# A linear-attention and MLP kernel: crossbar transposes moved to TensorE, w_in loaded through GpSimd's DMA queue with the cast in the transfer

## The chip, the cores and the metric

The kernel runs on one core of a Trainium2 chip. A core has TensorE (matrix products, PE in the profile, with its weight loads as PEld), VectorE (DVE), ScalarE (ACT), GpSimd (POOL) and SyncE (SP), which here only issues DMA transfers. The engines run side by side, each through its own list of instructions in the written order, and wait for each other through semaphores. TensorE writes to PSUM, of which this kernel uses eight banks; VectorE and ScalarE copy results from there to SBUF. The metric is the time of one execution on the device in microseconds.

## The reference

Two parts follow each other. The first is a linear attention with decay, over 4 batches, 8 heads, 768 steps and 48 features per head:

```python
for t in range(S):
    cur = np.einsum('bhd,bhe->bhde', u[None] * kt, vt)
    y[:, :, t] = np.einsum('bhd,bhde->bhe', rt, state + cur)
    state = wt[:, :, :, None] * state + np.einsum('bhd,bhe->bhde', kt, vt)
```

The second takes the 3072 rows of 384 that come out, as x, through an MLP with 2048 hidden features:

```python
h = x @ w_in
r = np.maximum(h, 0.0)
g = s * (r * r) + b
return g @ w_out
```

Inputs and output are float32. The kernel does its matrix products in bf16.

## The kernel before, in words

The 768 steps of each batch are cut into 6 chunks of 128, so there are 24 chunks, numbered 0 to 23; the number goes through the batches first, then through the steps. Chunks 0 to 3 are loaded and worked on in pairs ("packed", pkt tiles), the others alone (wt, rkt, vt tiles). The steps of one chunk, by the names that the written order uses:

- load n.0 to n.3: w, r, k, v come in over SP's DMA queue.
- ln, cum, exp, inc, exn: logarithm of w (ScalarE), its running sum (TensorE, L410 and others), exponentials (ScalarE), with inc on VectorE.
- mul: the products prd of r and k with these exponentials (VectorE, L489).
- The turn of prd, so that features lie across partitions. tr and tev: TensorE makes eight 128 x 128 transposes into PSUM (L538), and ScalarE or VectorE copies them to the tile RK (function move, L552 and L554). Or tev alone: a transposing DMA on SP (dtrans, L575), called the crossbar in this document, which needs neither TensorE nor a copy. `xbar_rk(n)` and `xbar_x(n)` choose by thresholds.
- mt, msk: scores (TensorE, L617) and their triangular mask (VectorE, L629).
- rkp, rku, cd, yd: the diagonal term with u. Two products on GpSimd (L346, L352), a sum on VectorE (L369), a product on GpSimd (L375).
- vb: v in bf16, by whichever engine the order names.
- dmm, sup, l2, st: the new state. TensorE (L741), VectorE (L784), GpSimd (L525, L793).
- ymm, yev: the chunk's output (TensorE, L667 and L676; VectorE, L758), which is a part of x.
- The turn of x: xtr and xev (three transposes on TensorE, L804, and a copy), or xev alone as a transposing DMA (dxtr, L585).

Two chunks make a tile of 256 rows of x; there are 12 tiles. For each, eight groups g1 T.i of six matmuls make 256 hidden features at a time (L858), relu (ScalarE, L871) and sq (ScalarE L881, VectorE L883) make gT, and g2 T.q sums over the hidden features in groups of four matmuls (L901). oev scales and adds a row that comes from b and the column sums of w_out (L912), and store writes it out.

The weights come in five pieces of 2, 2, 4, 4 and 4 times 128 hidden features. Before the change a piece of w_in is loaded by SP into a float32 staging tile (load_win, L826; li in the order) and cast to bf16 by ScalarE (pieces 0, 1, 3 in the list CIE; the order overrides it) or another engine (cast_in; ci in the order; L981, L983, L985). w_out goes the same way (load_wout L838, co), and its float32 staging tiles are also summed over rows for the output's constant (csred, csadd, cssplit). Staging tiles are shared: three large ones and two half-sized, for w_in and w_out together.

What sets the order of the work is the text ORDER: one list of words for all engines, worked through from front to back. Each engine gets its instructions in the order in which its words stand there. A word such as sq3.1@A names the operation, the tile or chunk, the part, and the engine that takes it (A, D, P for ScalarE, VectorE, GpSimd). A number such as +9 stands for so many matmuls on zeros (L1286, "fillers"), which keep TensorE running in the opening. Each PSUM tile of the ring psP (six banks: sums, scores, transposes, outputs, states, hidden features) can be written again only when its reader is done. SP's list works the same way: a load that has to wait for a buffer holds up everything behind it.

Of the kernel before, what the change touches and what calls it, by code (L numbers as in the profile page):

```python
# [18 lines left out]
CIE = 'AAPAP'  # L19
# [8 lines left out]
DTK = 9  # L28
DTX = 18
DK2 = 24  # L30
DX2 = 24
# [10 lines left out]
load0.0 load0.2 +9 load0.1 ln0 load2.2 cum0.0 load0.3 cum1.0 exp0.0 +1 u_mm exp0.1 load2.0 exp1.0  # L42
rkp0 mul0.0 load2.1 cum1.1 mul0.1 exp1.1 rkp1 load4.0 u_ev@D tr0 mul1.0 +4 tev0@A mul1.1 rku1 li0
tr1 load2.3 exl0 +2 rku0 cd1 tev1@A li1 ln2 cd0 mt0 load4.1 msk1.0 cum2.0 rkp3 l21 li2 msk0.0 +2 yd1
ln4 exp2.0 cum3.0 cum3.1 msk0.1 l20 rku3 ci0@A load4.2 msk1.1 cum4.0 +3 vb0@D vb1@A yd0 mul2.0
exp2.1 lo0 dmm0 exp3.1 mul2.1 +2 li3 exp3.0 li4 exl2 mul3.0 exp4.0 l23 cum4.1 sup0 vb3@P ymm0.0
exp4.1 tr2 rkp2 ci1@A mul3.1 st0 ymm0.1 sup1 ydm0 vb2@A l24 lo1 rku2 ymi0 yev0@D tr3 yev1@A tev2@D
xtr0 tev3@A xtr1 l22 +1 st1 xev0@D cd2 xev1@A mt2 cd3 rkp4 ci2@A g10.0 msk3.0 yd3 g10.1 msk2.0
relu0.0 lo2 msk2.1 yd2 ymm2.0 relu0.1 g10.2 msk3.1 rku4 dmm2 mul4 relu0.2 ymm2.1 ydm2 co0@A ci3@P
g10.3 sq0.1@A sup2 yev2@A cd4 st2 ymi2 sq0.2@A xtr2 sup3 yev3@A csred0@D lo3 g10.4 sq0.0@A ci4@D  # L50
load5.0 xev2@A xtr3 g10.5 load6.0 relu0.3 co1@D xev3@A lo4 g10.6 csred1@D sq0.3@A load5.1 g11.0
relu0.6 csadd1@D g11.1 relu0.4 co2@D relu0.5 g20.0 csred2@D sq0.4@A g10.7 sq0.6@A g11.2 sq0.5@A
relu0.7 g11.3 csadd2@D relu1.0 load5.2 g20.1 co3@D relu1.3 g20.4 relu1.1 load6.1 csred3@D ln5 g20.5
ln6 tr4 sq0.7@A cum6.0 csadd3@P tev4@D cum5.0 relu1.2 g11.4 inc6 sq1.3@A load6.2 g11.5 sq1.0@A co4@D
cum5.1 exp5.0 g11.6 small2 csred4@D exp5.1 load5.3 exp6.0 g20.6 exn6 g11.7 relu1.6 mul5 relu1.4
small g20.7 sq1.1@A load4.3 csadd4@D g20.2 relu1.7 load7.0 cssplit tr5 sq1.2@A load8.0 relu1.5 mul6
csspread g20.3 csevac load8.1 tev5@D vb5@P tr6 sq1.5@A rkp5 oev0.0 tev6@A mt4 load9.0 oev0.1 g21.4
l25 msk4.0 sq1.4@A rku5 load7.1 dmm5 g21.0 vb4@A msk5.0 g21.5 ln7 load7.2 sup5 rkp6 sq1.7@A msk4.1
cum7.0 st5 yd4 dmm4 load8.2 g21.1 load9.1 ln8 exp7.0 sup4 l26 cum8.0 cd5 st4 ymm4 ln9 msk5.1 yd5
g21.6 sq1.6@A inc7 load6.3 ymm5 exp8.0 st3 yev4 cum9.0 exn7 g21.7 yev5 rku6 inc8 xtr4 xtr5 g21.2  # L60
xev4@A load10.0 mul7 l27 xev5@A g21.3 exn8 load9.2 inc9 rkp7 g12.0 oev1.1 exp9.0 load9.3 g12.1 mul8
relu2.0 l28 relu2.1 load7.3 g12.2 cd6 l29 sq2.1@A sq2.0@D yd6 g12.3 load11.0 tr7 load10.1 exn9
oev1.0 relu2.2 g12.4 tev7@D vb6@P relu2.3 load8.3 g12.5 relu2.4 sq2.3@D mul9 sq2.4@A mt6 relu2.5
g22.4 msk7.0 store0.0 sq2.2@A vb7@P g12.6 msk6.0 sq2.5@A rkp9 load11.1 tev9 msk6.1 dmm6 g22.0
relu2.6 rku7 ln10 sup6 g12.7 load10.2 ln11 msk7.1 tr8 rku9 relu2.7 cd7 g22.1 sq2.7@A cum10.0 cd9
tev8@A load12.1 vb9@A dmm7 ymm6 rkp8 inc10 g22.5 rku8 yev6 load12.0 cum11.0 sup7 g22.6 yd9 xtr6
# [103 lines left out]
def kernel(  # L170
# [650 lines left out]

    def load_win(i):
        fs, f0 = PIECES[i], F0[i]
        half = fs == 2
        st = wst.tile([128, KT, fs * 128], FP32, name="wi_st", tag="wsh" if half else "wst", bufs=2 if half else 3)
        nc.sync.dma_start(  # L826
            out=st,
# [159 lines left out]
    def cast_in(i):  # L987
        cast(("ci", i), w_in_sb[i], w_in_st[i])
# [338 lines left out]
```

## Time and profile before

| What | Value |
|---|---|
| Median of 3 runs | 183.34 us (183.16 to 183.92) |
| Profiled execution, its own time | 183.5 us |
| Span of the profiled execution | 181.7 us |
| TensorE busy | 171.8 us, 1874 matmuls |
| VectorE, ScalarE, GpSimd busy | 142.8, 142.2, 105.0 us |
| First-layer matmuls (L858) | 576, 70.9 us busy |
| Second-layer matmuls (L901) | 400, 71.8 us busy |
| Transposing DMAs | 15 of r and k, 6 of x |
| Transposes on TensorE | 72 of r and k (9 chunks), 54 of x (18 chunks) |

The span runs from the first instruction to the last; the execution's own time is some 1.8 us more. In the rows of the profile, a line number names the place in the kernel, then come engine, operation, output and inputs, shapes and counts. Busy times of matmuls overlap: 54 matmuls of 219 ns each did not hold TensorE for 54 times 219 ns. How long a group holds the engine is read from where the next one starts.

### The profile page before, as it was taken

Reading aid. Unit: us, or ns where it says so; the run is one execution under the profiler, and the core shown is the slowest. Engines: PE = TensorE matmul, PEld = TensorE weight load, DVE = VectorE, ACT = ScalarE, POOL = GpSimd, SP = SyncE. Lnnn points to the kernel's source line nnn. Section 1 sums busy time; section 2 is a strip of 40 time slices with the busy share of each in tenths; the row PEclk is TensorE's granted clock in tenths of the full one; section 3 lists DMA queues with packets and bytes.
Section 4 is the critical chain, followed back from the end, with each engine's and each line's share of the span. In section 5 each row is a group of like instructions: output and inputs, shape, how many; then the busy total and the mean of one; then the engine's idle time right before and its main releaser. Section 6 shows DMA issues by size and latency. Waiting matters only on the chain.

```text
span 181.7 us, 4868 instructions
## 1 busy us (share of the span) xinstructions
PE 171.8 (95%) x1874; PEld 131.9 (73%) x1876; DVE 142.8 (79%) x257; ACT 142.2 (78%) x279; POOL 105.0 (58%) x139
## 2 busy tenths in 40 slices
PE   7989879998999989999999999999999999999993
PEld 2455669765686769688689688787877696888762
DVE  7679999999999979798998497898998976330222
ACT  3589899998889559979878899898896188479920
POOL 3889860229599699559869759289809560000000
PEclk9999999999999999999999999999999999999999
DMA  5999999999898998999989889999994794220013
GB/s 154 323 324 343 387 350 274 260 184 206 167 207 178 187 187 182 199 171 183 232 186 195 212 172 202 208 199 243 160 206 100 158 238 153 69 60 11 0 43 132
DMA packets 116554, 34.72 MB, mean 191 GB/s; under 512 B 110898, under 2 KB 114739, under 8 KB 116531
## 3 DMA queue, kind: packets, MB, share of 16 engines
q1 hardware_dynamic: 116528, 34.42, 81.6%
q8 instruction: 14, 0.23, 0.5%
q14 instruction: 10, 0.07, 0.1%
q10 hardware_dynamic: 2, 0.00, 0.0%
HBM read 25.17 MB, written 4.72 MB: 164 GB/s over the span
## 4 chain that ended last, share of the span: by engine, by line
PE 64%; DVE 10%; DMA 7%; POOL 6%; issue 5%; ACT 4%; SPq 1%; DVEq 0%; ACTq 0%; POOLq 0%
PE o_ps L901 27%; PE h_ps L858 26%; DMA wo_st<-in_moe_w_out_dram 4%; DMA rkt<-in_k_dram 3%; PE mt_ps L617 2%; POOL rkp L346 2%; PE y_ps L676 2%; DVE prd L489 2%; PE y_ps L667 2%; POOL rku L352 1%; POOL yd L375 1%; PE d_ps L741 1%; ACT rh L871 1%; PE cums L410 1%; PE xt_ps L804 1%
## 5 line engine op out<-in xcount | busy, mean ns | idle before, releaser
L901 PE MATMUL o_ps<-w_out,gT 128*128 128x384 bf16 (+2 forms) x400 | 71.8, 320 | 0.5 <-ACT gT L881 0.5
L858 PE MATMUL h_ps<-xT,w_in 128*128 128x256 bf16 x576 | 70.9, 273 | 1.1 <-POOL w_in L983 0.6
L871 ACT ACTIVATE rh<-h_ps 128x512 bf16<-128x512 f32 x96 | 54.4, 597 | 16.6 <-PE h_ps L858 15.7
L858 PEld LDWEIGHTS <-w_in 128*128 128x128 bf16 x576 | 59.9, 110 | 6.1 <-issue 1.0
L901 PEld LDWEIGHTS <-gT 128*128 128x128 bf16 x400 | 36.1, 98 | 19.7 <-ACT gT L881 0.7
L881 ACT ACTIVATE gT<-rh 128x512 bf16<-128x512 bf16 x78 | 47.4, 634 | 0.5
L352 POOL TENSOR_TENSOR rku<-rkp,u_bc 128x384 f32<-128x384 f32 x24 | 27.7, 1158 | 2.2 <-DVE cd L369 1.6
L346 POOL TENSOR_TENSOR rkp<-rkt 128x384 f32<-128x384 f32 x20 | 21.3, 1068 | 11.2 <-DMA rkt<-in_k_dram 9.4
L629 DVE TENSOR_TENSOR mt_sb<-mt_ps,tri_strict 128x512 bf16<-128x512 f32 x40 | 25.4, 681 | 1.9 <-PE mt_ps L617 1.8
L375 POOL TENSOR_TENSOR yd<-vt,cd 128x384 bf16<-128x384 f32 x20 | 17.6, 884 | 11.0 <-DVE cd L369 10.7
L489 DVE TENSOR_TENSOR prd<-rkt,E 128x768 bf16<-128x768 f32 x20 | 23.7, 1187 | 0.3 <-ACT E L473 0.3
L912 DVE SCALAR_TENSOR_TENSOR o_sb<-o_ps,s_bc,bconst 128x384 f32<-128x384 f32 (+2 forms) x25 | 14.6, 594 | 6.4 <-PE o_ps L901 6.3
L883 DVE TENSOR_TENSOR gT<-rh 128x512 bf16<-128x512 bf16 x18 | 9.6, 536 | 10.2 <-ACT rh L871 10.2
L793 POOL TENSOR_TENSOR st<-stmp,l 128x384 bf16<-128x384 bf16 x16 | 15.5, 972 | 0.8 <-DVE stmp L784 0.8
L758 DVE TENSOR_TENSOR x_sb<-y_ps,yd 128x384 bf16<-128x384 f32 x20 | 10.7, 549 | 5.3 <-PE y_ps L676 5.2
L369 DVE TENSOR_REDUCE cd<-rku 128x8 f32<-128x384 f32 x24 | 12.8, 542 | 1.4 <-POOL rku L352 1.4
L448 ACT ACTIVATE E<-cums 128x388 f32<-128x388 f32 (+1 forms) x22 | 10.4, 496 | 4.3 <-DVE inc L463 2.4
L784 DVE TENSOR_TENSOR stmp<-d_ps,st 128x384 bf16<-128x384 f32 x16 | 8.7, 550 | 3.2 <-PE d_ps L741 3.1
L473 ACT ACTIVATE E<-inc 128x384 f32<-128x384 f32 x18 | 9.3, 525 | 1.5 <-DVE inc L463 1.4
L1286 PE MATMUL warm_ps<-warm_sb 128*128 128x512 bf16 x22 | 7.7, 477 | 1.3 <-DVE warm_sb L1242 1.2
L983 POOL CAST vb<-vt 128x384 bf16<-128x384 f32 x9 | 5.6, 629 | 4.1 <-DMA vt<-in_v_dram 4.1
L676 PE MATMUL y_ps<-vb,mt_sb 128*128 128x48 bf16 x160 | 7.3, 183 | 0.0
(112 smaller groups left out, 200.6 us busy)
## 6 DMA issues: line engine op xcount, KB each, us to landing
wt<-in_w_dram SPq DMA_DIRECT2D x20, 192.0 KB, 3.9
rkt<-in_r_dram SPq DMA_DIRECT2D x20, 192.0 KB, 3.8
rkt<-in_k_dram SPq DMA_DIRECT2D x20, 192.0 KB, 3.7
vt<-in_v_dram SPq DMA_DIRECT2D x20, 192.0 KB, 3.6
out_dram<-o_sb SPq DMA_DIRECT2D x19, 192.0 KB, 3.0
wi_st<-in_moe_w_in_dram SPq DMA_DIRECT2D x3, 768.0 KB, 7.5
wo_st<-in_moe_w_out_dram SPq DMA_DIRECT2D x3, 768.0 KB, 7.0
pkt<-in_w_dram SPq DMA_DIRECT2D x2, 384.0 KB, 4.1
```

The source lines that it names most:

```text
L346: nc.gpsimd.tensor_tensor(out=rkp, in0=c["r"], in1=c["k"], op=ALU.mult)
L352: nc.gpsimd.tensor_tensor(out=rku.rearrange("t h d -> t (h d)"), in0=c["rkp"].rearrange("t h d -> t (h d)"), in1=u_bc, op=ALU.mult,)
L369: nc.vector.reduce_sum(out=cd, in_=c["rku"], axis=AX.X)
L375: nc.gpsimd.tensor_tensor(out=yd, in0=c["v"], in1=c["cd"].unsqueeze(2).to_broadcast([128, H, D]), op=ALU.mult,)
L489: nc.vector.tensor_tensor(out=prd[:, :, :, 0:D], in0=c["rk"], in1=c["E"][:, :, 0:HD].rearrange("t x (h d) -> t x h d", h=H), op=ALU.mult,)
L629: nc.vector.tensor_tensor(out=c["mt"][:, sg], in0=c["mt_ps"][sg], in1=(masks[:, n % 2] if packed(n) else tri_strict) .unsqueeze(1) .to_bro ...
L793: nc.gpsimd.tensor_tensor(out=c["st_new"], in0=c["stmp"].rearrange("q p (g e) -> q p g e", g=2), in1=c["l2"].unsqueeze(3).to_broadcast([12 ...
L858: nc.tensor.matmul(ps[:, f, :], lhsT=w_in_sb[PIECE[ft]][:, kt, :].rearrange("p (m j) -> p j m", j=PIECES[PIECE[ft]])[:, ft - F0[PIECE[ft]] ...
L871: nc.scalar.activation(out=rh, in_=hs[T, i], func=AF.Relu)
L881: nc.scalar.activation(out=g, in_=rh, func=AF.Square)
L901: nc.tensor.matmul(os_[T, k][:, cols], lhsT=gT[T][:, ft, tt * 128 : (tt + 1) * 128], rhs=w_out_sb[PIECE[ft]][:, ft - F0[PIECE[ft]], cols], ...
L912: nc.vector.scalar_tensor_tensor(out=o_sb[:, cols], in0=os_.pop((T, k))[:, cols], scalar=s_bc, in1=bconst[:, cols], op0=ALU.mult, op1=ALU.add,
```

## The change

Three things change.

1. The four thresholds of the crossbar are set to 99, above every chunk's number. All 24 chunks have r and k turned by TensorE, and all 24 parts of x. The transposing DMAs are gone.
2. A piece of w_in is loaded by GpSimd's DMA queue straight into the bf16 tile, the turn to bf16 done in the transfer. There is no staging tile for w_in and no cast; g1 waits for the transfer (li) itself. The staging tiles serve w_out alone.
3. The order is a new text. In it GpSimd may take squares (14 of the 96), and which engine makes which eviction, cast and square differs throughout.

```diff
-DTK = 9
-DTX = 18
-DK2 = 24
-DX2 = 24
+DTK = 99
+DTX = 99
+DK2 = 99
+DX2 = 99
...
     def load_win(i):
         fs, f0 = PIECES[i], F0[i]
-        half = fs == 2
-        st = wst.tile([128, KT, fs * 128], FP32, name="wi_st", tag="wsh" if half else "wst", bufs=2 if half else 3)
-        nc.sync.dma_start(
-            out=st,
+        nc.gpsimd.dma_start(
+            out=w_in_sb[i],
             in_=moe_w_in[:, f0 * 128 : (f0 + fs) * 128].rearrange(
                 "(kt p) f -> p kt f", p=128
             ),
         )
-        w_in_st[i] = st
...
         if pl.ops["sq", T, i]["eng"] == "ACT":
             nc.scalar.activation(out=g, in_=rh, func=AF.Square)
         else:
-            nc.vector.tensor_tensor(out=g, in0=rh, in1=rh, op=ALU.mult)
+            eng = nc.gpsimd if pl.ops["sq", T, i]["eng"] == "POOL" else nc.vector
+            eng.tensor_tensor(out=g, in0=rh, in1=rh, op=ALU.mult)
...
-    def cast_in(i):
-        cast(("ci", i), w_in_sb[i], w_in_st[i])
...
                 [("xev", CPT * T + j) for j in range(CPT)]
-                + [("ci", PIECE[i * FPQ])]
+                + [("li", PIECE[i * FPQ])]
...
-        add(("li", i), "SP", 0.8, load_win, (i,), [], [("wsh" if PIECES[i] == 2 else "wst", [("ci", i)])],
-            WIN_AT[i] + 0.01 * i, dma=2.15 * PIECES[i] / 4)
+        add(("li", i), "POOL", 1.0, load_win, (i,), [], [],
+            20.0, dma=2.15 * PIECES[i] / 4)
```

The opening of the order, before and after. In the new one w_in's loads stand among GpSimd's words, pieces 1 and 0 first, and four of the five loads of w_out (lo) stand ahead of chunk 4's r and k (load4.1, load4.2):

```diff
-load0.0 load0.2 +9 load0.1 ln0 load2.2 cum0.0 load0.3 cum1.0 exp0.0 +1 u_mm exp0.1 load2.0 exp1.0
-rkp0 mul0.0 load2.1 cum1.1 mul0.1 exp1.1 rkp1 load4.0 u_ev@D tr0 mul1.0 +4 tev0@A mul1.1 rku1 li0
-tr1 load2.3 exl0 +2 rku0 cd1 tev1@A li1 ln2 cd0 mt0 load4.1 msk1.0 cum2.0 rkp3 l21 li2 msk0.0 +2 yd1
-ln4 exp2.0 cum3.0 cum3.1 msk0.1 l20 rku3 ci0@A load4.2 msk1.1 cum4.0 +3 vb0@D vb1@A yd0 mul2.0
...
+load0.0 load0.1 +9 load0.2 load2.1 load2.3 ln0 cum0.0 exp0.0 exl0 mul0.0 u_mm load2.0 +1 cum1.0
+exp0.1 li1 load0.3 exp1.0 cum1.1 exp1.1 +3 rkp0 u_ev@D mul0.1 load2.2 tr0 mul1.0 vb2@A load4.0 li0
+rkp1 mul1.1 +2 lo3 tev0@D tr1 tev1@A +4 rku0 ln2 mt0 +2 cum2.0 vb3@A rku1 cd0 msk1.0 l20 cd1 exl2
+li2 lo0 vb1@A lo2 cum3.0 lo1 load4.1 l22 msk0.0 +2 load4.2 exp2.0 cum3.1 load5.0 yd0 +3 msk0.1
+mul2.0 vb0@A exp2.1 l21 dmm0 yd1 msk1.1 ln4 li3 +1 rkp3 mul2.1 exp3.0 sup0 cum4.0 st0 exp3.1 mul3.0
...
```

## The prediction

> **What bounds the kernel now.** I read the head of the page first, then its slices, to see which engine has no room.
>
> ```profile
> span 181.7 us, 4868 instructions
> ...
> PE 171.8 (95%) x1874; PEld 131.9 (73%) x1876; DVE 142.8 (79%) x257; ACT 142.2 (78%) x279; POOL 105.0 (58%) x139
> ...
> PE   7989879998999989999999999999999999999993
> ...
> PEclk9999999999999999999999999999999999999999
> DMA  5999999999898998999989889999994794220013
> ```
>
> TensorE is at nine tenths or more from the second quarter to the end, at full clock. The DMA row is as full up to slice 30, but a busy queue is only a bound if someone waits for it. Matmuls are pipelined, so a busy share hides gaps; I price TensorE by the distance between the starts of neighbouring groups. The timeline of TensorE, in the one place where both kinds of transpose stand close together, and two pieces of the chain that ended last:
>
> ```profile
> 53.50 0.61 PE L538 MATMUL trps<-shift,prd 128*128 128x128 bf16 x8
> 53.95 1.47 PE L858 MATMUL h_ps<-xT,w_in 128*128 128x256 bf16 x12
> ...
> 62.76 0.34 PE L804 MATMUL xt_ps<-shift,x_sb 128*128 128x128 bf16 x3
> 62.93 0.81 PE L901 MATMUL o_ps<-w_out,gT 128*128 128x384 bf16 x4
> 63.58 0.33 PE L667 MATMUL y_ps<-st,RK 128*128 128x96 bf16 x4
> ```
>
> ```profile
> 13.77 6.30 DMA rkt<-in_k_dram
> ...
> 27.55 6.97 DMA wo_st<-in_moe_w_out_dram
> 34.52 1.00 POOL wo_st L949
> ...
> 67.36 3.93 PE h_ps L858 x36
> ...
> 170.74 7.85 PE o_ps L901 x64
> 178.62 0.32 DVE o_sb L912
> ```
>
> Eight r/k transposes hold TensorE for 0.45 us (53.50 to 53.95), three x transposes for 0.17, four second-layer matmuls for 0.65; six first-layer ones take 3.93/6 = 0.655. The same way every unit of the written order gets its price: 96 first-layer groups 62.9, the second layer 62.4, 9 transposes of r/k 4.1, 18 of x 3.1, 24 fillers of 0.215 5.2, the rest (sums, scores, outputs, states) 30.0: 167.7 us. The span is 181.7, so TensorE streams nothing for 14.0 us. Where? Setting the ordered work against the time of the last first-layer matmul of a tile: tile 0 ends at 28.8 us with 24.2 of work done (4.5 idle); tile 2 at 59.3 with 50.7 (4.1 more); tile 3 at 73.0 with 63.3 (1.1 more); from there to 178.6 another 1.2; after the last matmul 3.1 (last eviction and store). So from 59 us on TensorE almost never waits: there each microsecond of work added to it lengthens the span.
>
> The other engines, in the three stretches cut at those times (us; busy of PE, PEld, DVE, ACT, POOL with counts; clock, DMA share, GB/s):
>
> ```profile
> 28.80:59.30 30.50, 28.99 (x297) 22.35 (x295) 29.50 (x45) 27.70 (x57) 18.23 (x22) 1.00 0.96 204
> 59.30:112.40 53.10, 52.43 (x599) 42.18 (x597) 44.75 (x81) 45.06 (x92) 41.66 (x51) 1.00 0.95 193
> 112.40:178.60 66.20, 66.02 (x659) 51.94 (x656) 43.89 (x78) 47.28 (x92) 24.39 (x27) 1.00 0.60 133
> ```
>
> In the first VectorE is full too (29.5 of 30.5), in the second the others have 15 to 20% of room, in the third much more.
>
> **The transposes.** The thresholds of 99 send chunks 9 to 23 (15) and x of chunks 18 to 23 (6) back to TensorE: 15 x 0.45 + 6 x 0.17 = 6.75 + 1.02 = 7.8 us. All stand behind tile 2's last first-layer group in the new order, where TensorE has no gaps to take them: +7.8. The Trainium skill speaks louder against this edit: "TensorE: Matmul & The Clock Gate", Part 4: PE-mode transpose, gives about 275 ns for one in a kernel and says that transposes don't count for the full clock. Worked out from it, 138 transposes would be an estimated 38 us. The row has 219 ns as the length of one but 0.056 as its pitch, and the clock stood at 1.00 while 126 of them ran; the row decides, 7.8.
>
> What leaves is SP's:
>
> ```profile
> RK<-prd SPq DMA_TRANSPOSE x15, 3.7
> ...
> L552 ACT COPY RK<-trps 128x1024 bf16<-128x1024 bf16 x5 | 5.0, 1008 | 1.7 <-PE trps L538 1.7
> L554 DVE COPY RK<-trps 128x1024 bf16<-128x1024 bf16 x4 | 2.7, 684 | 0.4 <-PE trps L538 0.2
> L793 POOL TENSOR_TENSOR st<-stmp,l 128x384 bf16<-128x384 bf16 x16 | 15.5, 972 | 0.8 <-DVE stmp L784 0.8
> ```
>
> SP's 15 issues of 1.3 to 2.1 us and 6 of 1.2 held up the loads and stores behind them, and the DMA share falls. After 60 us nobody waited for a load for long (TensorE 1.2 us for everything), so this frees nothing on the path: 0. If TensorE were not the bound, it would be worth at most those 1.2.
>
> **Evictions, casts and squares.** The new order has 12+12 r/k evictions on ScalarE/VectorE (before 5+4), 13+11 of x (11+7), all five w_out casts on ScalarE (1+4), no w_in casts (3 on ScalarE, 1 VectorE, 1 GpSimd), 65 squares on ScalarE (78), 17 on VectorE (18), 14 on GpSimd (none). With 1.01/0.68 us an r/k eviction, 0.48/0.35 of x, casts of 0.83 or 1.49 on ScalarE and 0.55 or 0.95 on VectorE, 0.63 a square on ScalarE: ScalarE +7.1 +1.0 -3.1 +5.3 -8.2 and 1.5 of small moves, +3.5; VectorE about +1. On 142 each, while the span grows by 8, that is hidden beside TensorE. If the cover goes, each late eviction holds one of six PSUM buffers and the group six places later waits.
>
> GpSimd's square is not in the trace. Nearest row: L793, two bf16 inputs, 972 ns for 384 columns, so 1.30 for 512; its fastest, 0.82, would give 1.09, its slowest, 1.54, 2.06. I take 1.30: 14 x 1.3 = 18.2. Ten of these come at tile 7 or later, where GpSimd is idle (none of its instructions ran after 150 us): 0. Late there would be the second layer's last group, but the last two GpSimd squares stand some 2 us of matmuls before their reader. The stretch that matters is tile 2's end to tile 6's. Before: 10 rkp, 11 rku, 9 yd, 10 states, 8 l, 3 casts, 46.1 us by mean durations. After: 13, 13, 12, 10, 8, 5 and 3 squares, 59.4, against 57.1 of TensorE's work (51.7 before). GpSimd goes from 78% of the stretch to the brink. By durations alone it overruns by 2.3; by the busy time really seen (41.66 for the 46.1: neighbours overlap) it needs 53.7 and fits. Between 0 and 2.3: +1.2. Late next: yd and the states, then the y matmuls of a later chunk, and TensorE works in order.
>
> **w_in by GpSimd's queue.** Off SP go five issues (0.43 to 1.46 us, median 0.90) and the waits of w_out loads for staging buffers. On GpSimd five issues come ahead of real work: one before rkp0, one before rkp1, the third behind rku1, two around rkp3. No row shows such an issue. Low end 0.4 each, as SP's fastest; high end 1.5; I take 0.9. Three precede yd0/yd1, whose products ended at 15.6 us before and were read at 17.2: 2.7 minus 1.6 of slack makes the first x, and the first-layer matmul of 20.1 us, 1.1 late. The skill speaks against it: "SBUF — State Buffer", section "SBUF: two separate sides", says that GpSimd can't write descriptors while VectorE runs a two-port instruction, 620 ns becoming 3100. At 2.5 us for each of the three, 7.5 more: the first group near 28 us. No run here shows it yet; VectorE's work then is mostly two-input products, so I take the row and keep the other as a rival.
>
> Against that: the cast of w_in held up TensorE by 0.6 us, and up to tile 2's end VectorE has 51.3 of work in place of 54.4. VectorE filled that stretch, so TensorE's 4.1 idle there can shrink by at most about 2.9; but w_out's loads now go ahead of chunk 4's r and k, which the chain waited 6.3 us for, and the bytes are the same. I take -1.1, so the head comes out even: 0. The bounds are -3 and +6. Three more fillers (0.65) lie in head waits: 0, or 0.65 if data were early.
>
> **Sum.** Span 181.7 + 7.8 + 1.2 + 0 = 190.7. The profiled execution took 183.5, 1.8 more than its span; the runs' median is 183.34, 1.6 above the span. So 192.3 us, 4.9% more.
>
> **Rivals.** (1) GpSimd sets the middle: squares at 2.06 put its list at 61.7 against 57.1, +4.6 in place of 1.2: 195.7. For it: rku at 1.16 on average where 1.00 is possible, so it already loses time. Against: its list can lag where buffers allow. (2) Starved descriptors: w_in late, +6: 198. (3) The head pays: VectorE's relief is taken in full and GpSimd fits: 181.7 + 7.8 - 2.9 + 1.6 = 188.2. For it: SP idled on staging buffers from 18 to 30 us, and GpSimd waited 8.6 us for w_out and 4.1 for v. (4) The other side: not slower, by one mechanism, an earlier start of the first layer. With all 6.4 us of idle between 28.8 and 178.6 taken back the span is still 183.1; the first group would have to start by 18.7 us in place of 20.1 to reach 181.7. Against: the w, r, k chain ahead of it is unchanged.
>
> **How the numbers follow.** Likeliest case 0.60, 192.3 (own range 190 to 194.5); (1) 0.16; (2) 0.08; (3) 0.13; (4) 0.03. From 188 to 197 leaves out half of (3), (4), half of (2) and the end of (1), under 2 in 10. A half per cent is what a measurement tells here. Only the best of (4) is faster by more: 0.02; same 0.01; slower 0.97.
>
> **What would show it.** r/k transposes x192 and x transposes x72 at the same pitch; TensorE's idle near 14 us; GpSimd near 125 us busy, its squares near 1.3; first-layer start 20 to 21.5; clock 1.00. Wrong if transposes cost over 0.1 us each in the stream, if first-layer groups wait for w_in past 30 us, or if TensorE waits for GpSimd's states in tiles 3 to 6.

## The result, and the profile after

The changed kernel takes 198.35 us (median of 3 executions, 197.32 to 199.91) against 183.34: a ratio of 1.082, interval 1.070 to 1.094. The forecast was 192.3 us with a range of 188 to 197, so the direction was right and the size was not: the time lies 1.35 us above the range. A second series on another chip gave 199.18 (198.41 to 199.79). The profiled execution took 197.32 us, with a span of 195.4.

The page of the kernel after, head and slices:

```profile
span 195.4 us, 5159 instructions
...
PE 182.8 (94%) x2017; PEld 141.1 (72%) x2017; DVE 147.8 (76%) x261; ACT 144.8 (74%) x279; POOL 119.3 (61%) x156
...
PE   7969586999998999999999999999999999999993
...
DMA  6999998999899899989969995102011002020013
```

TensorE's row has a 5 in its fifth slice (19.5 to 24.4 us), where the row of before has an 8. From the eighth slice on it is as full as before. DMA falls away after slice 25, where the row of before is full up to slice 30; the transposing DMAs are gone.

Setting the ordered work of TensorE, at the prediction's prices, against the end of each tile's last first-layer group, as the prediction did for the kernel before (differences are of unrounded values):

| At the end of | Before: time, work, idle (us) | After: time, work, idle (us) |
|---|---|---|
| tile 0 | 28.8, 24.2, 4.5 | 37.0, 26.4, 10.6 |
| tile 2 | 59.3, 50.7, 8.6 | 64.4, 51.4, 13.1 |
| tile 6 | 112.4, 102.4, 10.0 | 123.0, 108.5, 14.5 |
| tile 11 | 170.6, 159.8, 10.8 | 186.0, 170.1, 16.0 |
| the span | 181.7, 167.7, 14.0 | 195.4, 175.9, 19.5 |

So the span splits at tile 2's end. Up to there the new kernel is 5.1 us late, for which the prediction had 0. From there to the end it takes 131.0 us in place of 122.4, 8.6 more, for which the prediction had 9.0. Net, the whole error is in the opening; behind tile 2 two smaller ones cancel, as told below.

Executions more than 1.5% above the fastest of the same run (two of a_k4's four, one of a_k4u's, three of b_win56's) stand in the medians and ranges below, not in the ratios.

The three stretches that follow tile 0, by windows (us, busy of PE, PEld, DVE, ACT, POOL with counts; clock, DMA share, GB/s):

```profile
37.02:64.42 27.40, 26.46 (x274) 21.04 (x273) 24.73 (x45) 24.95 (x49) 17.98 (x24) 1.00 0.99 197
64.42:122.97 58.55, 58.02 (x697) 47.26 (x695) 51.45 (x87) 51.81 (x104) 52.86 (x61) 1.00 0.88 188
122.97:194.14 71.17, 68.45 (x700) 54.51 (x697) 41.78 (x76) 44.65 (x85) 24.53 (x29) 1.00 0.11 38
```

In the second, GpSimd is busy for 52.86 of 58.55 us and TensorE for 58.02: GpSimd is near the brink and does not set the pace. The groups that the prediction priced without a row, or by neighbours:

```profile
L881 POOL TENSOR_TENSOR gT<-rh 128x512 bf16<-128x512 bf16 x14 | 14.5, 1039 | 38.6 <-ACT rh L868 38.6
...
L539 PE MATMUL trps<-shift,prd 128*128 128x128 bf16 x192 | 14.7, 219 | 3.2 <-DVE prd L483 1.7
...
L553 ACT COPY RK<-trps 128x1024 bf16<-128x1024 bf16 x12 | 12.2, 1018 | 3.4 <-PE trps L539 3.4
...
w_in<-in_moe_w_in_dram POOLq DMA_DIRECT2D x3, 384.0 KB, 8.9
```

A square on GpSimd takes 1.04 us, not 1.30. The transposes are 192 at the same length, and their pitch is the same: 0.44 us for eight, from 148.29 to 148.73 in the timeline of TensorE:

```profile
148.29 0.61 PE L539 MATMUL trps<-shift,prd 128*128 128x128 bf16 x8
148.73 0.33 PE L668 MATMUL y_ps<-st,RK 128*128 128x96 bf16 x4
```

The opening, in the chain of waits of the kernel after:

```profile
9.46 3.15 DVE prd L483
...
19.08 2.43 DVE prd L483
21.50 0.48 DVE st L777
...
22.02 0.33 PE yp_ps L706 x4
```

The two products on VectorE at 9.46 and 19.08 us stand for 3.15 and 2.43 us. In the kernel before the same two took 1.01 and 0.71:

```profile
7.20 1.01 DVE L482 TENSOR_TENSOR prd<-pkt,E 128x384 bf16<-128x384 f32 x1
...
15.31 0.71 DVE L482 TENSOR_TENSOR prd<-pkt,E 128x384 bf16<-128x384 f32 x1
```

TensorE waits 1.7 and 1.8 us for what follows from them. The first first-layer group starts at 25.3 us, in place of 20.1.

The first of the two products also starts late, at 9.46 us, and part of that is TensorE's clock. By the trace's clock records the full clock begins at 10.5 us in this execution, against 4.9 in the kernel before. The mean granted clock, 0.999 here, does not show it, because it leaves out the time ahead of the first record. The work shows it: u_mm, the product that spreads u, takes 1.64 us here and 0.91 in a_fill (below), where the full clock begins at 5.8 us. Both kernels have the same instructions up to there, and a_fill starts the product at 8.18 us:

```profile
6.08 1.64 PE L996 MATMUL u_ps<-u_row,one_row 1*128 1x384 f32 x2
```

```profile
6.07 0.91 PE L996 MATMUL u_ps<-u_row,one_row 1*128 1x384 f32 x2
```

### The profile page after: what moved, and what is told of

The parts are those of the page before. It is cut to its first block, busy times and chain, and to the rows that moved or that the text cites. A ratio compares the mean times of both kernels' runs of the same rounds, so it can differ in the third digit from the quotient of the medians.

```text
span 195.4 us, 5159 instructions
## 1 busy us (share of the span) xinstructions
PE 182.8 (94%) x2017; PEld 141.1 (72%) x2017; DVE 147.8 (76%) x261; ACT 144.8 (74%) x279; POOL 119.3 (61%) x156
## 4 chain that ended last, share of the span: by engine, by line
PE 73%; ACT 14%; DVE 9%; issue 1%; ACTq 0%; DVEq 0%
PE h_ps L855 28%; PE o_ps L899 26%; PE trps L539 5%; ACT rh L868 3%; DVE prd L483 3%; ACT RK L553 3%; PE warm_ps L1279 3%; ACT gT L878 3%; ACT w_out L979 2%; PE xt_ps L805 2%; PE mt_ps L618 2%; PE y_ps L677 2%; DVE prd L490 1%; PE y_ps L668 1%; PE cums L411 1%
## 5 line engine op out<-in xcount | busy, mean ns | idle before, releaser
L899 PE MATMUL o_ps<-w_out,gT 128*128 128x384 bf16 (+2 forms) x400 | 72.6, 319 | 0.3 <-DVE gT L881 0.3
L878 ACT ACTIVATE gT<-rh 128x512 bf16<-128x512 bf16 x65 | 39.7, 635 | 0.4
L881 POOL TENSOR_TENSOR gT<-rh 128x512 bf16<-128x512 bf16 x14 | 14.5, 1039 | 38.6 <-ACT rh L868 38.6
L490 DVE TENSOR_TENSOR prd<-rkt,E 128x768 bf16<-128x768 f32 x20 | 22.7, 1133 | 5.9 <-ACT E L474 4.7
L347 POOL TENSOR_TENSOR rkp<-rkt 128x384 f32<-128x384 f32 x20 | 24.4, 1224 | 1.1 <-DMA rkt<-in_k_dram 1.1
L353 POOL TENSOR_TENSOR rku<-rkp,u_bc 128x384 f32<-128x384 f32 x24 | 24.6, 1030 | 0.4
L539 PE MATMUL trps<-shift,prd 128*128 128x128 bf16 x192 | 14.7, 219 | 3.2 <-DVE prd L483 1.7
L539 PEld LDWEIGHTS <-prd 128*128 128x128 bf16 x192 | 12.1, 98 | 5.8 <-DVE prd L483 1.9
L553 ACT COPY RK<-trps 128x1024 bf16<-128x1024 bf16 x12 | 12.2, 1018 | 3.4 <-PE trps L539 3.4
L1279 PE MATMUL warm_ps<-warm_sb 128*128 128x512 bf16 x27 | 10.0, 497 | 1.2 <-DVE warm_sb L1235 1.2
```

The lines of the kernel that those rows point to most:

```text
L347: nc.gpsimd.tensor_tensor(out=rkp, in0=c["r"], in1=c["k"], op=ALU.mult)
L353: nc.gpsimd.tensor_tensor(out=rku.rearrange("t h d -> t (h d)"), in0=c["rkp"].rearrange("t h d -> t (h d)"), in1=u_bc, op=ALU.mult,)
L490: nc.vector.tensor_tensor(out=prd[:, :, :, 0:D], in0=c["rk"], in1=c["E"][:, :, 0:HD].rearrange("t x (h d) -> t x h d", h=H), op=ALU.mult,)
L539: nc.tensor.matmul(ps[:, x * HP + p, :], lhsT=c["prd"][:, x, 2 * p : 2 * p + 2, :].rearrange("t h d -> t (h d)"), rhs=identity, is_transpo ...
L553: nc.scalar.copy(out=out, in_=in_)
L878: nc.scalar.activation(out=g, in_=rh, func=AF.Square)
```

## The experiments

A run's place in the argument is best seen in one table: where tile 2's last first-layer group ends, and what follows from there to the end of the span, in each run's profiled execution. The changed kernel's two profiled executions differ by 1.9 us there and by 0.2 behind it.

| Run | Time: median (lowest to highest), us | Tile 2 ends, us | Rest of the span, us |
|---|---|---|---|
| before | 183.34 (183.16 to 183.92) | 59.3 | 122.4 |
| after | 198.35 (197.32 to 199.91) | 64.4 | 131.0 |
| a_again (after once more) | 199.18 (198.41 to 199.79) | 66.3 | 131.2 |
| b_turns | 193.93 (193.44 to 194.53) | 60.2 | 131.5 |
| b_win | 189.50 (188.76 to 190.21) | 66.1 | 122.3 |
| b_issue | 187.02 (185.73 to 187.21) | 62.2 | 123.2 |
| b_winlate | 190.22 (189.23 to 190.58) | 66.3 | 122.6 |
| b_win56 | 193.95 (189.69 to 194.50) | 65.8 | 122.1 |
| b_winfill | 189.13 (188.91 to 189.90) | 66.0 | 122.1 |
| b_both | 200.90 (199.40 to 201.86) | 67.5 | 131.1 |
| a_umm | 198.87 (197.07 to 199.69) | 66.3 | 131.4 |
| a_lateli | 199.50 (199.01 to 200.04) | 66.3 | 131.3 |
| a_k4 | 198.89 (196.00 to 199.58) | 66.2 | 131.5 |
| a_k4u | 197.43 (195.86 to 200.67) | 63.2 | 130.6 |
| a_k5u | 202.52 (201.44 to 203.73) | 70.8 | 131.0 |
| a_k5uf | 200.60 (200.24 to 201.74) | 68.3 | 130.6 |
| a_dturn | 205.36 (205.26 to 207.60) | 66.2 | 137.4 |
| a_fill | 196.90 (196.54 to 197.14) | 64.5 | 130.5 |
| a_k4uf | 196.56 (195.78 to 197.11) | 63.2 | 130.6 |
| a_k4ufl | 196.41 (195.91 to 198.25) | 64.3 | 130.5 |

The rest of the span has two values: 122.1 to 123.2 us with the crossbar, 130.5 to 131.5 with turns by TensorE; a_dturn, which mixes the changed order with the crossbar, stands apart. All else happens before tile 2's end.

### Each half of the change alone, and both in the old order

b_turns is the kernel before with turns on TensorE only:

```diff
-DTK = 9
+DTK = 99
...
-g22.4 msk7.0 store0.0 sq2.2@A vb7@P g12.6 msk6.0 sq2.5@A rkp9 load11.1 tev9 msk6.1 dmm6 g22.0
+g22.4 msk7.0 store0.0 sq2.2@A vb7@P g12.6 msk6.0 sq2.5@A rkp9 load11.1 msk6.1 dmm6 tr9 tev9@A g22.0
```

Some words near the new turns (a relu, an exponential, a product, an output) moved by a few places with them.

> The kernel before, with the turns of r, k (15 chunks) and x (6 chunks) alone put on TensorE; w_in stays on SP's queue with its casts. Theory (TensorE is the bound, a turn costs its pitch, the other 6 us of the change are lost in its opening): 7.8 us of added TensorE work and nothing taken back, 191 to 192.5 us, first first-layer matmul near 20 us as before. Rival 1 (turns on TensorE stall it for their evictions, so that they are most of the 15 us): 195 to 198. Rival 2 (the turns are nearly free, the rest does the damage): under 187.

Measured: 193.93 us, ratio 1.055 (1.051 to 1.059), 10.0 us over the run of before beside it (184.09 us on that chip). Behind tile 2 it adds 9.1 us, for a priced 7.8. Added up there as distances between the starts of neighbouring groups, the turns of r and k hold TensorE for 6.7 us in place of 0.45 and those of x for 3.2 in place of 2.0: 7.5 us more, close to the price. The rest, about 1.6 us, is small waits of other groups, none above 0.6 us, for what VectorE and ScalarE hand over; one of them:

```profile
84.33 0.62 PE L618 MATMUL mt_ps<-RK 48*128 48x128 bf16 x16
85.34 0.62 PE L539 MATMUL trps<-shift,prd 128*128 128x128 bf16 x8 [0.38 <-DVE prd L490]
```

b_win is the kernel before with w_in alone by GpSimd's queue, no staging, no casts:

```diff
-        nc.sync.dma_start(
-            out=st,
+        nc.gpsimd.dma_start(
+            out=w_in_sb[i],
...
-l20 rku3 ci0@A load4.2
+l20 rku3 load4.2
```

The words li keep their places; they now stand in GpSimd's list in place of SP's.

> The kernel before, with w_in alone loaded by GpSimd's queue in bf16, no staging and no casts; crossbar turns and the written order kept. Theory (the transfer as such is harmless, the opening of the new order is the trouble): 181.5 to 184.5 us, first-layer start 19.5 to 21 us. Rival (GpSimd's descriptors, or the lock that it holds against VectorE while it issues, are what makes the opening late in any order): 186 to 190, first-layer start 23 us or later, VectorE's r and k products in the opening longer than 1.5 us.

Measured: 189.50 us, ratio 1.031 (1.025 to 1.036), where the step of the prediction had no change, and VectorE's relief even spoke for a gain. All of the loss, 6.8 us in the profiled execution, lies before tile 2's end. Its full clock begins at 5.1 us, about as early as in the kernel before, so a late clock at the start is not the cause here. So the loss that the prediction put at nothing appears with this half of the change alone, in the old order.

b_both has both changes in the old order, without the new order and without squares on GpSimd:

```diff
-rkp9 load11.1 tev9 msk6.1 dmm6 g22.0
+rkp9 load11.1 msk6.1 dmm6 tr9 tev9@A g22.0
...
-l20 rku3 ci0@A load4.2
+l20 rku3 load4.2
```

> The kernel before in its own order, with both changes: all turns by TensorE (a few words moved up by 1 to 7 places where a buffer asked for it), and w_in by GpSimd's queue. Neither the new order nor squares on GpSimd. If the two costs add up (10.0 for the turns, 5.4 for w_in): 199 to 200 us, and the new order of the changed kernel is worth 1 us at most. Rival: they overlap (turns fill the waits that w_in brings), 195 to 197.5, and the new order loses; or they multiply, over 202, and the new order wins something.

Measured: 200.90 us, ratio 1.096 (1.090 to 1.101). The two costs add, and a little more: 10.0 + 5.4 from 183.36 would be 198.8, and it is 2.1 over that. So the new order is not where the 15 us come from. Whether it gains anything over the old one, with its squares on GpSimd, is not clear of noise: the changed kernel has 1.082 (1.070 to 1.094) and 1.087 (1.081 to 1.093).

### What w_in by GpSimd costs: the issues

b_issue keeps w_in on SP, casts and all, and adds five small transfers to GpSimd's queue at the places of li:

```diff
+    def load_scr(i):
+        f0 = F0[i]
+        nc.gpsimd.dma_start(
+            out=scr[i],
+            in_=moe_w_in[:, f0 * 128 : f0 * 128 + 16].rearrange(
+                "(kt p) f -> p kt f", p=128
+            ),
+        )
...
-dmm0 exp3.1 mul2.1 +2 li3 exp3.0 li4 exl2
+dmm0 exp3.1 mul2.1 +2 li3 gi3 exp3.0 li4 gi4 exl2
```

> The kernel before with five small transfers added to GpSimd's queue, at the places where the changed one loads w_in: 128x3 runs of 16 columns each into a scratch tile that nobody reads. w_in itself is staged by SP and cast as before. Theory Q (GpSimd's queue: the issues, some 4.3 us in all, stand ahead of its products for chunks 2 and 3, whose masks TensorE waits for): the second product of chunk 2 ends 2 to 4 us later than before (18.6 us), and the time is 187 to 190 us, most of what w_in by GpSimd cost. Rival T (the transfer: w_in's traffic and its late landing): without the bytes the loss is at most 1.5 us, 183.3 to 185.

Measured: 187.02 us, ratio 1.019 (1.015 to 1.023): of b_win's 5.4 us, 3.7 come with no bytes of w_in on that queue and no change to the casts. The five issues take 0.78 to 0.93 us each, ahead of GpSimd's products, and they reach TensorE by more than one way. The longest of its waits in the opening is for VectorE's cast of v, vb, in b_issue:

```profile
15.84 2.10 DVE L996 CAST vb<-pkt 128x384 bf16<-128x384 f32 x1
...
17.99 0.52 PE L726 MATMUL d_ps<-vb,prd 64*128 64x96 bf16 x16 [1.77 <-DVE vb L996]
```

and the same cast in the kernel before, where that wait is 0.4 us:

```profile
14.23 0.69 DVE L985 CAST vb<-pkt 128x384 bf16<-128x384 f32 x1
```

The first issue delays a product rku on GpSimd. VectorE works in order: its sum cd waits for rku, the masks stand behind cd, and the cast behind the masks; then the cast takes 2.10 us. Why it takes so long was not tested. About 0.9 us of its late start is there before any issue: in this execution TensorE's full clock begins at 6.7 us, against 4.9, and the product that starts at 7.20 us in the kernel before starts at 8.10, as long as there.

The second way runs through chunks 2 and 3. GpSimd's timeline in b_issue, then VectorE's:

```profile
18.57 1.57 POOL L838 DMA_DIRECT2D scr<-in_moe_w_in_dram  x2
...
21.90 0.99 POOL L352 TENSOR_TENSOR rku<-rkp,u_bc 128x384 f32<-128x384 f32 x1
```

```profile
22.92 1.01 DVE L369 TENSOR_REDUCE cd<-rku 128x8 f32<-128x384 f32 x2 [0.70 <-POOL rku L352]
23.85 2.48 DVE L629 TENSOR_TENSOR mt_sb<-mt_ps,masks 128x512 bf16<-128x512 f32 x4
```

rku of chunk 2 starts at 21.90 us in place of 17.63; cd waits for it, and the four masks of chunks 2 and 3, which TensorE needs, stand behind cd. TensorE's wait there is 0.6 us in b_issue and 1.9 in b_win. A third wait, 1.1 us for GpSimd's own cast of w_in (0.6 before), has no counterpart in b_win, which has no such cast. The prediction looked at yd0 and yd1 as the readers of late GpSimd work and found 1.6 us of slack; in the old order it overlooked cd, which had about half a microsecond for chunks 2 and 3 (the product ended at 18.64 us, cd began at 19.14). The changed kernel's order puts these two cd behind the masks, so there the second way is closed.

b_winlate moves the last two issues of b_win behind rku2:

```diff
-dmm0 exp3.1 mul2.1 +2 li3 exp3.0 li4 exl2
+dmm0 exp3.1 mul2.1 +2 exp3.0 exl2
...
-l24 lo1 rku2 ymi0
+l24 lo1 rku2 li3 li4 ymi0
```

> The kernel before with w_in by GpSimd's queue, and the last two of the five issues moved behind the product of chunk 2 that they delayed. Theory Q: that product ends 1.5 us earlier (20.7 in place of 22.3 us), TensorE's wait for the masks falls from 1.9 to 0.4 us, and 187 to 188.5 us. Rival T: the two pieces land some 3 us later, TensorE waits for them in tile 0, and the time is 190 us or more.

Measured: 190.22 us, no better than b_win. cd of chunks 2 and 3 started at 20.63 us in place of 22.30, as the first theory asked, but TensorE now waited 1.8 us for w_in and 1.8 for yd. Moving these two issues back does not mend it: their pieces are late then.

### The transfer: two queues on the same DMA engines

The changed kernel has w_in's bytes on that queue as well. a_lateli is the changed kernel with its first two issues moved behind GpSimd's products of chunks 0 and 1, so that these products would be done when VectorE's starts:

```diff
-exp0.1 li1 load0.3
+exp0.1 load0.3
...
-load4.0 li0 rkp1
+load4.0 rkp1
...
-rku1 cd0
+rku1 li1 li0 cd0
```

> The changed kernel, with GpSimd's first two w_in transfers issued behind its four products of chunks 0 and 1 in place of ahead and between. Theory[...]: GpSimd's products end 1.7 us earlier, near 10.5 us, VectorE's product of 3.1 us falls to 1 to 1.7, first-layer start 23.5 to 24.5 us, time 196 to 197.5. Rival (GpSimd's place doesn't matter, the clock does): no shorter product and the same time, 198 to 199.5.

Measured: 199.50 us, no gain, though VectorE's first product fell from 3.14 to 0.82 us and the first layer started at 23.1 us in place of 25.3. That the moved issues shortened the product is not shown. In a_fill they stand where the changed kernel has them, and the product is short too:

```profile
8.18 0.74 DVE L483 TENSOR_TENSOR prd<-pkt,E 128x384 bf16<-128x384 f32 x1 [0.27 <-ACT E L440]
```

What goes with its length is the clock at the start: full from 5.5 to 6.1 us in a_umm, a_fill and a_lateli, where the product takes 0.68 to 0.82 us, and from 10.5 and 17.1 in the two executions of the changed kernel, where it starts over a microsecond later, beside GpSimd's row of products, and takes 3.15. a_lateli's chain of waits tells what holds it up instead:

```profile
13.60 17.41 DMA rkt<-in_k_dram
...
31.13 0.97 DVE prd L490
...
32.15 0.62 PE trps L539 x8
```

Chunk 4's k took 17.41 us to land. In the kernel before the prediction shows the same load at 6.30 us. For some 8 of the 17 us, up to 21 or 22 us, w_out's four pieces, 2.3 MB, stood ahead of it in SP's queue. What slows it behind them, the DMA view of the changed kernel shows, from 24 to 28 us; the row after it is the kernel before's, in the same four microseconds:

```profile
DMA packets 1286, 0.77 MB, mean 192 GB/s; under 512 B 662, under 2 KB 1283, under 8 KB 1286
...
q0 software_dynamic: 638, 0.64, 93.4%
q1 hardware_dynamic: 648, 0.13, 28.2%
```

```profile
q1 hardware_dynamic: 300, 1.28, 90.5%
```

q0 is GpSimd's queue, q1 SP's. In the changed kernel 638 packets of w_in and 648 of SP's queue went through: one for one. In a_lateli it was 963 and 961 from 22 to 28 us, and in the changed kernel 251 and 251 from 18 to 22 us, when SP's packets were w_out's large ones. A packet of w_in writes 1024 bytes of bf16 (2048 read, 96 ns in the trace), one of chunk 4's k only 192. So SP's queue moved 0.13 MB in those four microseconds, a tenth of what it moved in the kernel before; there, however, its packets were large (1.28 MB in 300), so a fairer comparison is with 8 to 10 us in the kernel before, when SP's queue alone moved 1722 packets of some 380 bytes at 325 KB/us. At 648 packets in 4 us, a load of 192 KB, 1024 packets, needs an estimated 1024 / 648 x 4 = 6.3 us, for what the queue alone would do in an estimated 0.6. The Trainium skill says that transfers issued by several engines run on the same 16 DMA engines and interleave ("DMA: Bandwidth & Descriptors", section "Issuing engines are not separate DMA queues"); in these stretches they did so packet by packet, whatever the packets' sizes. Not in all stretches: in a_again SP's queue moved 119 packets to 383 of w_in from 26 to 28 us, in a_k5u 966 to 323 from 16 to 18. Nor does the cast in the transfer save the engines time: 96 ns for a packet with 2048 bytes read, where the staged load's packet of 2048 took 84 (medians of the traces).

a_k4 is a_lateli with chunk 4's r and k ahead of w_out in SP's queue:

```diff
-load4.0 rkp1 mul1.1 +2 lo3 tev0@D
+load4.0 load4.1 load4.2 rkp1 mul1.1 +2 lo3 tev0@D
...
-lo1 load4.1 l22 msk0.0 +2 load4.2 exp2.0
+lo1 l22 msk0.0 +2 exp2.0
```

> The changed kernel with li1 and li0 moved behind rku1 (as in the run of that name), and besides with chunk 4's loads of r and k ahead of the four pieces of w_out in SP's queue. Theory S (the two queues share the DMA engines packet by packet: for each packet of w_in, 1024 bytes written, SP's queue gets one of 192 bytes, so chunk 4's k took 17.4 us to land and TensorE waited 3.0 us for its product): k lands within 8 us, that wait goes, and 195.5 to 197.5 us in place of 199.5. Rival: w_out, now later, takes the place of that wait, and the time stays at 198.5 to 200.

Measured: k landed after 7.6 us, and TensorE's 3.0 us wait for chunk 4's product was gone; in its place TensorE waited 3.4 us for ScalarE. On the time the run decides nothing: its four executions took 196.00, 198.24, 199.55 and 199.58 us, on both sides of theory and rival (ratio 1.076, 1.066 to 1.086). Nor does it tell waiting behind w_out apart from sharing with w_in, as the loads now escape both.

a_k4u, with u_mm behind cum1.1 besides, shows what ScalarE was waiting for. a_umm is that move alone in the changed kernel:

```diff
-exl0 mul0.0 u_mm load2.0 +1 cum1.0 exp0.1 li1 load0.3 exp1.0 cum1.1
+exl0 mul0.0 load2.0 +1 cum1.0 exp0.1 li1 load0.3 exp1.0 cum1.1 u_mm
```

> The changed kernel, with the float32 product that spreads u (two matmuls with one active row, 1.6 us at the slow clock) moved behind the running sums of chunk 1. Theory (it held up the sums, the exponential and with them VectorE's product past the point where GpSimd shuts it out): E of chunk 0 ready 1 to 2 us earlier, the 3.1 us product of VectorE back to about 1, first-layer start 22 to 23.5 us in place of 25.3, time 195 to 196.5. Rival (the slow clock alone made the opening late): start within 0.5 us of what the same clock gives in the changed kernel, time 197.5 to 199.

> The same, and u_mm behind cum1.1 (as in the run of that name). Theory: the two edits of the start add a little to the one of the queue: 194 to 197 us. Rival: no better than without u_mm's move, 195.5 to 199.

Measured: a_umm 198.87 us, no gain clear of noise (TensorE waited 4.1 us for chunk 4's product), a_k4u 197.43. The chain of a_k4u:

```profile
15.16 16.16 DMA wt<-in_w_dram
...
31.34 0.53 ACT logw_two L342
```

The next small load, chunk 5's w, has taken the place of chunk 4's k: 16.16 us to land. a_k5u puts it ahead of w_out too:

```diff
-load4.0 load4.1 load4.2 rkp1
+load4.0 load4.1 load4.2 load5.0 rkp1
```

> The run with chunk 4's loads early and u_mm moved (197.4), and chunk 5's w load as well ahead of w_out: it had taken 16.2 us to land. Theory S: ScalarE's wait for it and the two waits of TensorE behind it (1.4 and 0.7 us) go: 195 to 196.5 us. Rival: the next small load (chunk 6's w, chunk 5's r) or w_out takes the place: 197 to 198.

Measured: 202.52 us, 5 us worse than a_k4u where 1 to 2.5 better was expected. Its chain:

```profile
14.17 5.54 SPq L836
...
21.30 11.00 DMA wo_st<-in_moe_w_out_dram
...
32.32 0.83 ACT w_out L979
```

With three small loads at its head, SP's queue crept from 14 to 20 us: the first w_out issue alone stood 5.54 us, and w_out came so late that ScalarE's cast held up the first layer. The expectation was wrong in taking the delay for that of one load: in a_lateli, a_k4u and a_k5u the queue was late as a whole, and whichever load stood behind paid.

b_win56 asked in the old order whether small loads (chunks 5 and 6's w) make up what b_win loses beyond b_issue:

```diff
-rku3 load4.2 msk1.1
+rku3 load4.2 load5.0 load6.0 msk1.1
```

> The kernel before with w_in by GpSimd's queue, and the w loads of chunks 5 and 6 ahead of w_out in SP's queue, behind chunk 4's k. Theory S (starved small loads make the 2.5 us between this transfer and its issues alone): 187 to 188.3 us in place of 189.5. Rival: w_out's own lateness, or VectorE at half speed beside GpSimd, makes them, and the time stays at 189 to 190.5.

Measured: 189.69 us at best and 193.95 at the median, no better than b_win at either. The spread, at nearly the same clock (0.97 to 0.98), is not explained, and the run gives the theory no support. What makes those 2.5 us in the old order stays open. They arise behind tile 0, which ends at 32.8 us in b_win and 33.05 in b_issue. Seen in b_win's timeline there, not tested, are VectorE's instructions beside GpSimd's products of chunks 5 and 6, from 39.6 us on: a cast of w_out takes 1.80 us (0.95 elsewhere), a sum 3.08 (1.55 in b_issue), and TensorE waits 2.3 us for a product behind them. In b_issue GpSimd still waits for v at that time. The last w_out issue stands 9.4 us.

### TensorE's clock

b_winfill adds fillers to b_win at its two long waits:

```diff
-lo2 msk2.1 yd2 ymm2.0
+lo2 msk2.1 yd2 +8 ymm2.0
...
-load7.0 cssplit tr5
+load7.0 cssplit +10 tr5
```

> The kernel before with w_in by GpSimd's queue, and 8 and 10 fillers in the written order at the two places where TensorE waited about 2 us for VectorE (ahead of the y matmuls of chunk 2, and of the turns of chunk 5). Theory C (each of the two waits brings a 3.41 us stretch of half clock, worth 1.7 us of work): the clock stays full, and the time falls by 2.5 to 3.5 us to 186 to 187. Rival: the clock's half stretches are made up within the waits that follow, and the time stays at 189 to 190.5.

Measured: 189.13 us, ratio 1.032 against b_win's 1.031. The granted clock rose from 0.98 to 0.99 in b_win's executions to 1.00 in all four, and the time stayed: there the rival held. a_fill does the same to the changed kernel:

```diff
-mul0.1 load2.2 tr0
+mul0.1 load2.2 +4 tr0
...
-mul3.1 ymi0
+mul3.1 +8 ymi0
...
-load4.3 tr4
+load4.3 +6 tr4
```

> The changed kernel with 18 fillers more in TensorE's order: 4 ahead of chunk 0's and 1's turns, 8 ahead of the y matmul that waits for chunk 0's state, 6 ahead of chunk 4's turns. Theory C (half stretches of the clock, 3.41 us each, cost 1.5 us apiece, and differ from execution to execution): the clock is 0.99 or more in all executions and the times stand at 196.5 to 198, against 197.3 to 199.9. Rival: the clock fills but the waits keep their ends, as in the order of before: 198.4 to 199.5.

> The changed kernel as it is, once more, beside the next three. 197.3 to 199.9 us as before; chunk 4's k, on SP's queue behind four pieces of w_out and beside w_in on GpSimd's queue, lands some 16 us after its issue again; VectorE's product of chunk 1 with two inputs stands about 3 us again.

Measured: a_fill 196.54 to 197.14 us at a clock of 0.991 in all four executions, ratio 1.074 (1.067 to 1.080); the changed kernel, once more, 198.41 to 199.79 at 0.980 to 0.991, ratio 1.087 (1.081 to 1.093). Eighteen fillers, 3.9 us of work for TensorE, cost nothing and go with a gain of 1.5 us over the first series, where the intervals of the ratios overlap, and of 2.3 over the second, where they do not. What made it is not shown. The mean clock alone does not: one execution of a_again took 199.43 us at the same 0.991. And in a_fill's profiled execution the clock came up early, before the first of these fillers ran, and one half-clock stretch, from 19.5 to 22.9 us, stayed. In a_again's profile the clock is full only from 17.1 us, and half again from 23.9 to 27.3.

These stretches are 3.41 us long or multiples of it; the Trainium skill gives the window as 3413 ns, free-running, with half or full clock and nothing between ("TensorE: Matmul & The Clock Gate", Part 1), and the runs agree in the length. The kernel before had a mean of 0.998 to 1.000 in every execution beside these runs; the changed one had 0.999, 0.980 and 0.982 in the first three. Of a_again's other two expectations one was half right, chunk 4's k landing after 12.9 us in place of some 16, and one right: VectorE's product stood 3.15 us again.

### VectorE beside GpSimd

a_k4uf is a_k4u with fillers, a_k4ufl the same with li3 and li4 behind rkp2; a_k5uf is a_k5u with the same fillers:

```diff
-mul3.1 ymi0
+mul3.1 +8 ymi0
...
-ln5 g20.0
+ln5 +6 g20.0
```

and in a_k4ufl, over a_k4uf:

```diff
-msk1.1 ln4 li3 +1 rkp3
+msk1.1 ln4 +1 rkp3
...
-+8 ymi0 li4 ydm0
++8 ymi0 ydm0
...
-rkp2 tr3
+rkp2 li3 li4 tr3
```

> The run with chunk 4's loads early, li1 and li0 behind rku1 and u_mm behind cum1.1 (197.4), with 8 fillers ahead of the y matmul that waits for chunk 0's state and 6 ahead of the second layer's first group. Theory C: the clock stays at 0.99 or more and the times stand together at 195 to 196.5 us. Rival: no gain, 197 to 198.

> The same, with the last two w_in issues moved behind chunk 2's first product on GpSimd. Theory V (VectorE's product with two inputs stands while GpSimd issues and multiplies back to back): the second such product takes 0.7 in place of 2.4 us, chunk 0's state comes 1.7 us earlier, the first layer starts at 20.5 in place of 22.2 us; the time falls by 1 to 1.7 us, unless w_in's last pieces, some 3 us later, are then waited for. Rival: the product stands all the same beside GpSimd's product, and the late pieces cost 1 to 2 us.

> The same with 8 fillers ahead of the y matmul that waits for chunk 0's state and 6 ahead of the second layer's first group. Theory C: no half stretches, 194.5 to 196 us, all executions within 1 us. Rival: no gain over the run without them.

The second of VectorE's blocked products, in a_k4uf and in a_k4ufl:

```profile
15.61 2.42 DVE L483 TENSOR_TENSOR prd<-pkt,E 128x384 bf16<-128x384 f32 x1
```

```profile
15.67 1.29 DVE L483 TENSOR_TENSOR prd<-pkt,E 128x384 bf16<-128x384 f32 x1
```

Without the issues beside it the product takes 1.29 us in place of 2.42, and TensorE's wait for chunk 0's state falls from 1.8 to 0.7 us. So GpSimd's issues themselves hold VectorE up, by 1.1 us here, in one execution of each. But the time is the same, 196.41 against 196.56, as the expectation's caveat had it: w_in's last pieces come later and TensorE waits 2.4 us for ScalarE. By their ratios the fillers gained nothing clear of noise in a_k4uf (1.070, 1.063 to 1.077, against a_k4u's 1.075, 1.068 to 1.082), and a_k5uf, 200.60 us, is 2 us under a_k5u, not the 6 expected. a_k4uf and a_k4ufl are, with a_fill, the best of the changed kernel's repairs, and still 2.5 us slower than b_turns, which leaves w_in where it was.

### One run that did not tell what it was made for

a_dturn gives the turns of chunks 9 to 23 back to the crossbar, in the changed kernel's order:

```diff
-DTK = 99
+DTK = 9
...
-tr8 mul9 rku8
+tr8 mul9 rku8 tev9
...
-yev6 tr9 yd7
+yev6 yd7
...
-load17.0 tev9@D rkp10
+load17.0 rkp10
```

> The changed kernel in its order, w_in by GpSimd's queue, with the turns of chunks 9 to 23 and of x 18 to 23 given back to the DMA crossbar, issued by SP up to 12 words ahead of where TensorE turned them (chunks 9 to 19) or at that place. If the turns cost just their work on TensorE (7.8 us predicted): 190 to 191.5 us. Rival: as much as between the runs in the order of before (10.0 to 11.4): 187 to 188.5. Second rival: this order, written for turns by TensorE, waits for the crossbar, and little is gained: over 193.

Measured: 205.36 us, slower still, as the second rival had it: TensorE waited 6.4 us for the crossbar's results, because the order asks for them too early. It prices nothing but the fit of an order to its transport; the price of the turns is b_turns'.

## Why the prediction was wrong

- **Turns, +7.8.** Right: the turns themselves hold TensorE for 7.5 us more behind tile 2 in b_turns, with the pitch of the row confirmed (0.44 to 0.45). Around them come some 1.6 us of small waits, which the prediction put at nothing, 9.1 us in all. The price of 38 us that the prediction set aside was far off.
- **GpSimd at the brink, +1.2.** It did not come. Squares took 1.04 us, not 1.30, GpSimd was busy 119.3 us, not 125, and TensorE did not wait for it in tiles 3 to 6. With the waits around the turns the sum behind tile 2 came out at 8.6 for a predicted 9.0: two errors that cancel, which is luck.
- **The head, 0.** This step failed: w_in by GpSimd's queue was to come out even, +1.1 for three issues and -1.1 for VectorE's relief. Measured is +5.1 us in the profiled execution up to tile 2's end, and +5.4 in time with that half of the change alone, in the old order (b_win). The issues' length was right (0.9 predicted, 0.78 to 0.93 measured), their readers were not. It counted three issues and yd0 and yd1 behind them; all five together go with 3.7 us in the old order (b_issue), most of it by waits for VectorE, which works in order behind late GpSimd products. "The bytes are the same" was the other wrong sentence: on a second queue the same bytes take packets' turns from SP's small loads (17.4 us for a load that took 6.3, part of it behind w_out). How the 5.1 us of the changed kernel divide between issues, packets, clock and the new order is not shown. The bound of +6 in the prediction did hold; it was weighed too low.
- **VectorE's relief, -1.1.** Not shown. Between tiles 0 and 2 the changed kernel needs 27.4 us in place of 30.5, but b_win, with the same relief in the old order, needs 33.4; so the relief alone does not make the 27.4, and no run parts it from the new order.
- **Clock 1.00.** Wrong: a mean of 0.98 to 0.99 in most executions, and a late start of the full clock in both profiles of the changed kernel. Nothing in the sum stood for it. What it costs is not settled: fillers went with 1.5 to 2.3 us less in a_fill and with nothing in b_winfill.
- **Three more fillers, 0.** They cost nothing that shows, as eighteen more did in a_fill.
- **Rivals.** (2), starved descriptors, gave 198 us, the number measured, by another mechanism. That is luck: it wanted issues of 2.5 us; they stayed at 0.93 or less, and VectorE was the one that stood. (1) fell because GpSimd did not set the middle, (3) and (4) because the opening paid: the first layer starts at 25.3 us, where 20 to 21.5 was expected and (4) needed 18.7.
- **What stays open:** the 2.5 us between b_win and b_issue in the old order, and how the changed kernel's opening divides. Its parts don't add up one by one: each repair handed the time to the next wait, and no run has the new order with w_in left on SP's queue, which would part the two.

## What to carry to other kernels

When a transfer moves to an engine's own queue, price its issues as instructions of that engine, and follow every in-order reader behind them, not the nearest one. Then count packets: where two queues went packet for packet, as here in the stretches shown, a bulk load with large packets left a queue of small ones 0.13 MB in four microseconds, and everything behind them on that queue was late. Look at when TensorE's full clock begins in each profiled execution before comparing two openings: here it moved by over ten microseconds between executions, and a product on another engine, 3.15 us long or 0.74, went with it.

## What the runs showed of the hardware

- Two DMA queues went packet for packet where both had work: 638 packets of 1024 bytes written and 648 mostly of 192 bytes in 4 us, at 192 GB/s in all; 963 and 961 in 6 us of a_lateli. Some stretches of a_again and a_k5u were uneven.
- Casting in the transfer did not shorten it: 96 ns a packet with 2048 bytes read and 1024 written, 84 ns for a plain one of 2048.
- VectorE's product of two SBUF operands stood through a row of GpSimd's products. VectorE's line and GpSimd's, in the changed kernel:

```profile
9.46 3.14 DVE L483 TENSOR_TENSOR prd<-pkt,E 128x384 bf16<-128x384 f32 x1 [1.14 <-ACT E L440]
```

```profile
9.27 1.01 POOL L347 TENSOR_TENSOR rkp<-pkt 128x384 f32<-128x384 f32 x1
10.22 1.95 POOL L353 TENSOR_TENSOR rku<-rkp,u_bc 128x384 f32<-128x384 f32 x2
12.13 0.53 POOL L526 TENSOR_TENSOR l<-lamp,par 128x8 f32<-128x8 f32 x1
12.61 0.80 POOL L825 DMA_DIRECT2D w_in<-in_moe_w_in_dram  x1
```

  The product ends at 12.60 us, when that row of GpSimd's instructions ends. The Trainium skill says that whichever of the two starts first has the shared ports for its whole instruction ("SBUF — State Buffer", section "SBUF: two separate sides"). Here VectorE, which came second, did not get them between GpSimd's instructions either; in a_k4ufl it did: the product ran from 15.67 to 16.96 us while two GpSimd products in a row ran from 15.55 to 17.81.
- Half-clock stretches of 3.41 us, or multiples of it, came after waits of about 2 us (25.6 to 29.0 us in b_win, after a wait of 1.89 us that ended at 24.56), and not in every execution of a kernel. The full clock began between 4.2 and 17.1 us after the start of the span, in different executions.
